# Third expert block in float32r halves, and weight conversions moved out of its steps into the second pair

## The chip, the cores and the metric

One Trainium2 chip, one of its cores. The metric is the device time of one execution in microseconds. The engines are named as the profile names them: PE (TensorE, matmuls), PEld (its weight loads), DVE (VectorE), ACT (ScalarE), POOL (GpSimd) and SP (SyncE, which here issues most transfers).

## What is computed

Clustered attention, then a mixture of eight experts with the best expert for each token, then one more pair of matmuls with a leaky ReLU:

```python
mask = q_assign[:, :, :, None] == k_assign[:, :, None, :]
attn = softmax(where(mask, q @ k.T / 8, -1e9))
x = (attn @ v) as (1536 tokens, 512)
for e in range(8):
    xe = x[expert_idx == e]
    out[expert_idx == e] = gate_w * (relu(xe @ w1[e]) @ w2[e])
h = out @ w_in
y = (relu(h) + alpha * min(h, 0)) @ w_out
```

w1 and w2 are 512x1024 and 1024x512 for each expert, w_in and w_out 512x2048 and 2048x512. All in float32.

## The kernel before, in words

The program has three stretches: attention (to about 258 us in the trace), the experts (258 to 438 us) and the second pair of matmuls (438 us to the end).

**The experts** run as 64 steps, g = 0 to 63, eight to a block. A block is one expert with a fixed number of columns (tokens), `CAPS = (208, 306, 216, 200, 192, 176, 168, 128)`. In step g the loop of line 1307 issues, in this order: `l1` of block g // 8 and slice f = g % 8 of the 1024 hidden units (four products over d), `l2` of the slice two steps back (`LAG = 2`; four products, one for each quarter o of the output), at the end of a block `y_evac` (the four sums leave PSUM), then side work of the step (a small table, lines 1117 to 1150), the entries of `ahead`, the token load of the next block (`x_load`, a transfer that ACT issues), register loads, the transposes of the next block's tokens (`x_transp`, at f = 6), and last a conversion where the table `CONV` has one. Each engine takes its instructions in this order.

**Products.** Blocks other than the second are float32: one product is two records on PE. The second block (`HB = 1`, 306 columns) is in float32r halves: each operand is a rounded high half and a low half (the rest), and `thrice` adds up high times high, high times low and low times high, three records of one pass each. The halves of the weights are made by `wsplit` two steps ahead: one ACT copy of 512 columns makes the high half, one DVE subtraction the low half, into six buffers in turn. The halves of the tokens are made in `x_transp`, those of the hidden units in `l1` (ACT ReLU, DVE subtraction out of PSUM).

**Conversions.** The weights of the second pair arrive as 64-bit floats and are turned into float32 piece by piece. A conversion of one piece (`conv_step`) is four DVE operations of 512 columns (`conv_bits`, lines 178 to 181), each working on the one before, then the store of the piece before, the ACT operation that begins the next piece (`conv_begin`, line 174), and the load of a later piece. `CONV` names the 26 steps that have one; eight of them are in steps 16 to 24. Pieces 3 to 5 are made in place: `conv_begin` of one writes into the area that the raw piece before it is still read from.

**Weights** of the experts come by `wload` through a ring of four 1 MB slots, issued by SP, after `l1` and `l2` of slices 3 and 7.

**The second pair** is 16 rounds of about 15.8 us. A round has seven products `prod` (a Strassen scheme, operands in float32r halves) and twelve groups of three matmuls (`second`, line 1393) on the round before. DVE and ACT make sums and halves of weights for the next round, activations and their halves. `xt_next(r, place)` puts work of the second half of tokens at four places of a round.

Of the kernel before, what the change touches and what calls it, by code (L numbers as in the profile page):

```python
# [21 lines left out]
P = 128  # L22
# [8 lines left out]
E = 8  # L31
# [60 lines left out]
def tile_cluster_attention_moe(ctx: ExitStack, tc: tile.TileContext, qk, kk, v, cen, cenr, gate, mw, m2w,  # L92
# [73 lines left out]
    n1, n2 = iter(range(NPW, NF)), iter(range(NF, 2 * NF))  # L166
    NEARLY = 6
    seq = [next(n2) for _ in range(NEARLY)]
    while len(seq) < 2 * NF - NPW:
        seq += [next(n2), next(n1)]  # L170
# [5 lines left out]
    def conv_bits(t, raw):  # L176
        ti = t.bitcast(I32)
        nc.vector.tensor_scalar(t, t, float(np.ldexp(1.0, -15)), None, ALU.max)
        nc.vector.tensor_scalar(ti, ti, 3, 0x3FFFFFFF, ALU.logical_shift_left, ALU.bitwise_and)
        nc.vector.scalar_tensor_tensor(ti, raw[:, :, 0], 29, ti, ALU.logical_shift_right, ALU.bitwise_or)  # L180
        nc.vector.scalar_tensor_tensor(ti, raw[:, :, 1], -0x40000000, ti, ALU.bitwise_and, ALU.bitwise_or)
# [720 lines left out]
    HB = 1  # L902
# [77 lines left out]
    def x_transp(blk, half=None):  # L980
        nt, np_ = parts(blk)
        nb = nt * np_
        xr = xrt[blk]
        if half != 1:
# [5 lines left out]
        x = xts[blk]  # L990
# [18 lines left out]
    worder = [(0, 0), (0, 1), (0, 2), (1, 0), (0, 3), (1, 1), (0, 4), (1, 2), (0, 5), (1, 3), (0, 6), (1, 4), (0, 7), (1, 5),  # L1009
              (1, 6), (1, 7)]  # L1010

    def wsplit(layer, f):
        b = wbuf[worder.index((layer, f)) % 6].rearrange("p (h d f) -> p h d f", h=2, d=4)
        w = wslots[4 * HB + 2 * (f // 4) + layer]
# [6 lines left out]
        split[layer, f] = b  # L1021

    def thrice(ps, w, i, hi, lo, start, stop):
        nc.tensor.matmul(ps, w[:, 0, i, :], hi, start=start, stop=False)  # L1024
        nc.tensor.matmul(ps, w[:, 0, i, :], lo, start=False, stop=False)  # L1025
        nc.tensor.matmul(ps, w[:, 1, i, :], hi, start=False, stop=stop)  # L1026

    def l1(blk, f):
# [6 lines left out]
        for d in range(4):  # L1035
            if blk == HB:
                thrice(ps, split[0, f], d, x[:, d, :], split["x"][:, d, :], d == 0, d == 3)
# [7 lines left out]
        if f % 4 == 3:  # L1045
            wload()

    def l2(blk, f):
# [6 lines left out]
        for o in range(4):  # L1055
            y = yps[blk][o][:, 0:nb]
            if blk == HB:
                thrice(y, split[1, f], o, h, split["h"][f % 4], f == 0, f == 7)
            else:
                nc.tensor.matmul(y, w[:, f % 4, o * P:(o + 1) * P], h, start=f == 0, stop=f == 7)  # L1060
        if f % 4 == 3:
            wload()

    def y_evac(blk, col):
        nb = CAPS[blk]
        for o, y in enumerate(yps.pop(blk)):
            dst = (x2a if o < 2 else x2b)[:, o % 2, col]
            if o % 2 == 0:
# [128 lines left out]
    def s_half(r, n):  # L1197
# [10 lines left out]
        else:  # L1208
# [22 lines left out]
    for g in range(7, 16):  # L1231
        for v in (8, 9) if g == 7 else (g + 2,):
            for layer, f in ((0, v - 8), (1, v - 10)):
                if 0 <= f < 8:
                    ahead.setdefault(g, []).append(lambda layer=layer, f=f: wsplit(layer, f))
# [423 lines left out]
```

## Time and profile before

| | us |
|---|---|
| median of 3 runs | 696.54 (695.32 to 697.29) |
| the profiled execution | 696.02 |
| its span, first to last instruction | 694.2 |
| PE busy | 679.9 (98%) |
| DVE busy | 478.9 (69%) |
| ACT busy | 378.3 (54%) |

The span has a start time for every instruction. On PE a record's duration runs past the start of the next one, so the pace of PE is read from start to start and not from the durations. On DVE and ACT an instruction's time covers its write, and the next independent one starts a little before it ends. A bracket at the end of a row is idle time ahead of the instruction and what ended it.

### The profile page before, as it was taken

What the parts mean: (1) busy time and instruction counts of PE and PEld (TensorE: products, weight loads), DVE (VectorE), ACT (ScalarE), POOL (GpSimd) and SP (SyncE); (2) the same over time, 40 slices, a digit from 0 to 9 for tenths busy, and PEclk for the clock granted to TensorE, in tenths of its full rate; (3) what the DMA queues carried; (4) which work ended last, traced back from release to release, by engine and by line L of the source; (5) the groups of instructions that cost most, each with busy time, mean ns of one, the idle gap of its engine ahead of it and who ended that gap; (6) DMA issues with size and microseconds to landing.
All of it is one profiled execution on the core that took longest, in us unless ns stands there. A gap on an engine that the chain in (4) does not pass through costs nothing.

```text
span 694.2 us, 11439 instructions
## 1 busy us (share of the span) xinstructions
PE 679.9 (98%) x4149; PEld 573.4 (83%) x4149; DVE 478.9 (69%) x885; ACT 378.3 (54%) x747; POOL 61.5 (9%) x67
## 2 busy tenths in 40 slices
PE   9999999999999999999999999999999999999994
PEld 3677667767766699999999999898899889998983
DVE  8777778777797667687747663777788765445552
ACT  6777877767776517433333443655556564334441
POOL 3220202220040130000000000000000030000003
PEclk9999999999999999999999999999999999999998
DMA  8446886633254335668999989553334565554412
GB/s 257 121 161 178 294 293 224 221 113 87 86 152 156 112 132 180 196 209 246 357 360 315 354 279 278 165 195 140 136 137 152 197 212 176 151 158 138 151 31 93
DMA packets 49145, 131.78 MB, mean 190 GB/s; under 512 B 8398, under 2 KB 14053, under 8 KB 44895
## 3 DMA queue, kind: packets, MB, share of 16 engines
q1 hardware_dynamic: 44424, 115.85, 51.1%
q0 software_dynamic: 3216, 12.60, 5.1%
q10 hardware_dynamic: 1447, 2.58, 1.5%
q8 instruction: 34, 0.56, 0.4%
q14 instruction: 24, 0.20, 0.1%
HBM read 98.15 MB, written 30.24 MB: 185 GB/s over the span
## 4 chain that ended last, share of the span: by engine, by line
PE 56%; DMA 2%; ACT 1%; DVE 1%; issue 1%; POOL 0%; POOLq 0%; ACTq 0%; DVEq 0%
PE PS L1261 16%; PE PS L1060 9%; PE PS L1039 9%; PE PS L1397 6%; PE PS L1396 6%; PE PS L1395 6%; DMA w<-in_mw 2%; PE PS L1026 1%; PE PS L1024 1%; PE PS L1025 1%; PE PS L998 1%; POOL out_dram L1408 0%; ACT gc L1377 0%; DVE SHL L1166 0%; DVE gc L1380 0%
## 5 line engine op out<-in xcount | busy, mean ns | idle before, releaser
L446 ACT ACTIVATE P<-PS,sm 128x768 f32<-128x768 f32 x96 | 86.5, 901 | 29.6 <-DVE sm L436 29.4
L436 DVE TENSOR_REDUCE sm<-PS 128x1 f32<-128x768 f32 x96 | 91.9, 957 | 14.4 <-PE PS L430 13.9
L460 PEld LDWEIGHTS PS<-cst,P 128*128 128x128 f32 x576 | 63.4, 140 | 28.7 <-ACT P L446 15.6
L460 PE MATMUL PS<-cst,P 128*128 128x128 f32 x576 | 81.7, 277 | 0.5 <-ACT PT L462 0.2
L1039 PE MATMUL PS<-x,w 128*128 128x208 f32 (+6 forms) x448 | 79.2, 320 | 0.9 <-ACT h L1041 0.9
L1060 PE MATMUL PS<-h,w 128*128 128x208 f32 (+6 forms) x448 | 79.1, 319 | 0.4 <-DMA w<-in_mw 0.4
L463 DVE COPY PT<-PS 128x384 f32<-128x384 f32 x96 | 53.0, 553 | 34.4 <-PE PS L460 34.2
L1397 PE MATMUL PS<-BH,gc 128*128 128x512 f32 x192 | 75.8, 395 | 0.0
L1396 PE MATMUL PS<-BL,gc 128*128 128x512 f32 x192 | 75.5, 393 | 0.0
L1395 PE MATMUL PS<-BH,gc 128*128 128x512 f32 x192 | 75.1, 391 | 0.0
L429 PE MATMUL PS<-KA,QA 128*128 128x512 f32 x192 | 73.6, 384 | 0.0
L1039 PEld LDWEIGHTS PS<-x,w 128*128 128x128 f32 x448 | 71.5, 190 | 1.5 <-ACT h L1041 1.2
L469 PE MATMUL PS<-PT,V 128*64 128x384 f32 (+1 forms) x432 | 72.4, 462 | 0.0
L1060 PEld LDWEIGHTS PS<-h,w 128*128 128x128 f32 x448 | 71.8, 190 | 0.6 <-DMA w<-in_mw 0.6
L1261 PE MATMUL PS<-xT,SHL 128*128 128x384 f32 x336 | 68.2, 338 | 0.2 <-DVE gc L1493 0.2
L1261 PEld LDWEIGHTS PS<-xT,SHL 128*128 128x128 f32 x336 | 59.6, 188 | 4.9 <-DVE gc L1493 0.7
L462 ACT ACTIVATE PT<-PS 128x384 f32<-128x384 f32 x96 | 46.8, 487 | 28.2 <-PE PS L460 26.6
L430 PE MATMUL PS<-KB,QB 96*128 96x512 f32 x192 | 61.1, 339 | 0.0
L1041 ACT ACTIVATE h<-PS 128x208 f32<-128x208 f32 (+7 forms) x64 | 21.4, 334 | 57.3 <-PE PS L1039 49.2
L1261 PE MATMUL PS<-xB,SHL 128*128 128x384 f32 x240 | 48.5, 337 | 0.0
L1408 POOL DMA_INDIRECT out_dram<-row,PGR x12 | 11.7, 973 | 415.6 <-ACT row L1405 406.0
L469 PEld LDWEIGHTS PS<-PT,V 128*64 128x64 f32 x432 | 25.8, 136 | 23.9 <-issue 20.7
(277 smaller groups left out, 1142.9 us busy)
## 6 DMA issues: line engine op xcount, KB each, us to landing
w<-in_mw SPq DMA_DIRECT2D x32, 1024.0 KB
SS<-SHL SPq DMA_DIRECT2D x24, 512.0 KB
SHL<-SS SPq DMA_DIRECT2D x24, 512.0 KB
raw<-in_m2w SPq DMA_DIRECT2D x20, 512.0 KB
bwr<-WB SPq DMA_DIRECT2D x16, 512.0 KB
R<-in_qk SPq DMA_DIRECT2D x7, 768.0 KB
KA<-in_kk POOLq DMA_DIRECT2D x7, 768.0 KB
Xs<-in_zeros SPq DMA_DIRECT2D x8, 614.4 KB
```

What stands on the lines that cost most here:

```text
L429: nc.tensor.matmul(ps[:, ks], st["QA"][:, hh, q0:q0 + P], st["KA"][:, hh, ks], start=True, stop=False)
L430: nc.tensor.matmul(ps[:, ks], st["QB"][0:96, hh, q0:q0 + P], st["KB"][0:96, hh, ks], start=False, stop=True)
L436: nc.vector.tensor_reduce(smt[s], psS[s % 2], AX.X, ALU.max, negate=True)
L446: nc.scalar.activation(Pt, psS[s % 2], AF.Exp, bias=smt.pop(s)[:, 0:1], accum_out=RS[:, tt, h:h + 1])
L460: nc.tensor.transpose(v4[:, kt // 3, kt % 3, :], Pt[:, kt * P:(kt + 1) * P], idf)
L469: nc.tensor.matmul(psO[64 * hh:64 * hh + 64, qs], V[:, kt, 64 * hh:64 * hh + 64], PTs[u][:, hh, kt, qs], start=kt == 0, stop=kt == KT - 1)
L1039: nc.tensor.matmul(ps, w[:, d, fs], x[:, d, :], start=d == 0, stop=d == 3)
L1060: nc.tensor.matmul(y, w[:, f % 4, o * P:(o + 1) * P], h, start=f == 0, stop=f == 7)
L1261: mm = lambda d, h, x, first, last: nc.tensor.matmul(ps, SHL[:, h, i, d, :], x[:, d, :], start=first and start, stop=last, skip_group_chec ...
L1395: nc.tensor.matmul(y, gh[n][:, i, c], whi, start=start, stop=False)
L1396: nc.tensor.matmul(y, gh[n][:, i, c], wlo, start=False, stop=False)
L1397: nc.tensor.matmul(y, gl[n][:, i, c], whi, start=False, stop=last)
```

## The change

The third block (`JB = 2`, 216 columns) is put into float32r halves too. The high and low halves of its moving operand lie side by side, so that one record of 432 columns multiplies the high weights with both, and a second record of 216 columns multiplies the low weights with the high half (`both`). The PSUM bank then holds two parts that are added outside PE, in `j1` and in `y_evac`. Six conversions leave steps 16 to 24; two are placed anew at 47 and 55, the one at 57 goes, and the last five are cut into three parts each (lines 178 and 179; 180; 181 and what follows it) and put into rounds 1 to 5 of the second pair. Expert weights of blocks 1 and 2 are loaded as soon as `wsplit` has read a slot, and the register for their address is read one step earlier. The diff, cut to its core:

```diff
+    later = [n2[13], n1[-2], n2[14], n1[-1], n2[15]]
+    seq = n2[:NEARLY]
+    for a, b in zip(n2[NEARLY:13], n1):
+        seq += [a, b]
+    seq += n1[13 - NEARLY:-2]
+    NCE_ = len(seq)
+    seq += later
...
+    def conv_part(k, i):
+        conv_bits(cvt[k], raws[k], i)
+        if i == 2:
+            conv_next(k)
...
+        if blk == JB:
+            split["j"] = [t.rearrange("p (h n) -> p h n", h=2)
+                          for t in [wq_[:, 3072:3072 + 2 * nb]] + [t[:, 1024:1024 + 2 * nb] for t in wqx]]
...
+            elif blk == JB:
+                for k in range(dn):
+                    xj = split["j"][dn * g + k]
+                    nc.scalar.activation(xj[:, 0], pv[:, k], AF.Copy)
+                    nc.vector.tensor_sub(xj[:, 1], pv[:, k], xj[:, 0].bitcast(F32))
...
+    def wsplit(blk, layer, f):
+        b = wbuf[wcount[0] % 6].rearrange("p (h d f) -> p h d f", h=2, d=4)
+        wcount[0] += 1
+        w = wslots[4 * blk + 2 * (f // 4) + layer]
...
+        split[blk, layer, f] = b
+        if f % 4 == 3:
+            wload()
...
+    def both(ps, w, i, hl, start, stop):
+        n = hl.shape[-1]
+        nc.tensor.matmul(ps, w[:, 0, i, :], hl.rearrange("p h n -> p (h n)"), start=start, stop=False)
+        nc.tensor.matmul(ps[:, 0:n], w[:, 1, i, :], hl[:, 0], start=False, stop=stop)
+
+    def j1(f):
+        nb = CAPS[JB]
+        ps = bank(f % 2)[:, 0:2 * nb]
+        for d in range(4):
+            both(ps, split[JB, 0, f], d, split["j"][d], d == 0, d == 3)
...
+        nc.scalar.activation(h, ps[:, nb:2 * nb], AF.Copy)
+        nc.vector.tensor_add(h, ps[:, 0:nb], h)
+        nc.scalar.activation(hj[:, 0], h, AF.Relu)
+        nc.vector.scalar_tensor_tensor(hj[:, 1], h, 0.0, hj[:, 0].bitcast(F32), ALU.max, ALU.subtract)
+
+    def j2(f):
...
+        for o in range(4):
+            both(yps[JB][o][:, 0:2 * nb], split[JB, 1, f], o, split["hj"][f % 3], f == 0, f == 7)
...
+            if blk == JB:
+                nc.scalar.activation(dst, y[:, nb:2 * nb], AF.Copy)
+                nc.vector.tensor_add(dst, y[:, 0:nb], dst)
...
-    CONV = {1: 1, 2: 1, 10: 1, 13: 1, 16: 1, 17: 1, 18: 1, 19: 1, 20: 1, 21: 1, 22: 1, 24: 1, 25: 1, 27: 1, 28: 1, 30: 1,
-            32: 1, 34: 1, 36: 1, 38: 1, 40: 1, 43: 1, 45: 1, 49: 1, 52: 1, 57: 1}
+    CONV = {g: 1 for g in (1, 2, 10, 13, 18, 21, 25, 27, 28, 30, 32, 34, 36, 38, 40, 43, 45, 47, 49, 52, 55)}
...
+    for b_, first_ in ((HB, ((0, 7), (1, 7))), (JB, ())):
+        for f in range(8):
+            for layer in range(2):
+                g = dict(first_).get(f, 8 * b_ + f - 2) if layer == 0 else 8 * b_ + f
+                ahead.setdefault(g, []).append(lambda a=(b_, layer, f): wsplit(*a))
...
+            (j1(f) if blk == JB else l1(blk, f))
...
+            (j2(f2) if b2 == JB else l2(b2, f2))
...
+            if f == (0 if blk else 1) and blk + 1 < NB:
+                wreg[blk + 1] = reg(wi[0:1, blk + 1:blk + 2], [ET.SP], 4 * (E - 1))
...
+    late_at = {(1, 2): (0, 0), (1, 3): (0, 1), (1, 4): (0, 2), (2, 2): (1, 0), (2, 3): (1, 1), (2, 4): (1, 2),
+               (3, 2): (2, 0), (3, 3): (2, 1), (3, 4): (2, 2), (4, 1): (3, 0), (4, 2): (3, 1), (4, 3): (3, 2),
+               (5, 1): (4, 0), (5, 2): (4, 1), (5, 3): (4, 2)}
...
     def xt_next(r, place):
+        if (r, place) in late_at:
+            n, i = late_at[r, place]
+            conv_part(NCE_ + n, i)
```

## Rows read from the trace of the kernel before

**Rows 1.** The page, busy time, share of the span and instructions of each engine.
```profile
PE 679.9 (98%) x4149; PEld 573.4 (83%) x4149; DVE 478.9 (69%) x885; ACT 378.3 (54%) x747; POOL 61.5 (9%) x67
```
**Rows 2.** Waits of PE, experts (first), second pair (second): us, times, longest.
```profile
PE PS L1039 <- ACT h L1041: 0.9, 1, 0.9
...
PE PS L1261 <- DVE gc L1493: 0.2, 1, 0.2
```
**Rows 3.** Windows, steps 10-15, 16-23, 24-26: length, PE, PEld, DVE, ACT, POOL, PEclk, DMA.
```profile
286.78:308.06 21.28, 21.28 (x154) 21.27 (x153) 17.14 (x46) 9.83 (x21) 0.00 (x0) 1.00 0.81 256
308.06:332.74 24.68, 24.68 (x147) 24.48 (x146) 19.10 (x42) 8.69 (x20) 0.00 (x0) 1.00 0.75 240
332.74:341.07 8.33, 8.33 (x49) 8.33 (x49) 5.67 (x12) 2.96 (x8) 0.00 (x0) 1.00 0.98 357
```
**Rows 4.** Timeline of PE in the third block: start, us, engine, line, operation.
```profile
323.26 1.62 PE L1039 MATMUL PS<-x,w 128*128 128x216 f32 x8
...
326.18 1.62 PE L1039 MATMUL PS<-x,w 128*128 128x216 f32 x8
```
**Rows 5.** Timeline of PE: float32r records of 256, 306, 512 columns; transposes (L460).
```profile
150.49 0.28 PE L429 MATMUL PS<-KA,QA 128*128 128x256 f32 x1
150.61 0.29 PE L430 MATMUL PS<-KB,QB 96*128 96x256 f32 x1
150.74 0.82 PE L460 MATMUL PS<-cst,P 128*128 128x128 f32 x6
151.31 0.48 PE L429 MATMUL PS<-KA,QA 128*128 128x512 f32 x1
...
290.33 0.30 PE L1024 MATMUL PS<-x,wqx 128*128 128x306 f32 x1
290.47 0.30 PE L1025 MATMUL PS<-xlo,wqx 128*128 128x306 f32 x1
...
443.22 0.40 PE L1395 MATMUL PS<-BH,gc 128*128 128x512 f32 x1
443.46 0.39 PE L1396 MATMUL PS<-BL,gc 128*128 128x512 f32 x1
```
**Rows 6.** Groups by line and form, 255 to 445 us: busy us, mean ns | idle before.
```profile
L1020 DVE TENSOR_TENSOR wq<-w,wq 128x512 fp32r<-128x512 f32 x9 | 5.9, 684 | 1.6 <-ACT wq L1019 1.5
L1019 ACT ACTIVATE wq<-w 128x512 fp32r<-128x512 f32 x9 | 5.3, 622 | 0.0
L1041 ACT ACTIVATE h<-PS 128x216 f32<-128x216 f32 x8 | 2.7, 336 | 2.1 <-PE PS L1039 2.1
L1071 DVE COPY x2a<-PS 128x216 f32 x1 | 0.4, 383 | 2.0 <-PE PS L1060 2.0
```
**Rows 7.** Timeline of DVE, step 17: a conversion, the table of step 18, the next conversion.
```profile
315.09 0.42 DVE L178 TENSOR_SCALAR wA<-wA 128x512 f32<-128x512 f32 x1
...
317.35 0.23 DVE L1144 TENSOR_TENSOR tabr<-tabr,g 11x88 f32<-11x88 f32 x1
...
318.64 0.43 DVE L178 TENSOR_SCALAR cv<-cv 128x512 f32<-128x512 f32 x1 [0.38 <-issue]
```
**Rows 8.** Timeline of ACT, DVE and PEld around the start of step 16 (308.06).
```profile
306.01 0.66 ACT L174 ACTIVATE wA<-wA 128x512 f32<-128x512 f32 x1 [5.48 <-DVE wA L181]
306.58 0.42 ACT L1041 ACTIVATE h<-PS 128x306 fp32r<-128x306 f32 x1
...
307.54 0.69 DVE L1020 TENSOR_TENSOR wq<-w,wq 128x512 fp32r<-128x512 f32 x1
308.15 0.60 DVE L1007 COPY x<-PS 128x432 f32<-128x432 f32 x1
...
308.80 0.66 PEld L1039 LDWEIGHTS PS<-x,w 128*128 128x128 f32 x4 [0.16 <-DVE x L1007]
```
**Rows 9.** Windows of DVE, second pair, a round each: length, DVE busy, PEclk, DMA share.
```profile
490.67:506.50 15.83, 11.77 (x21) 1.00 0.43 153
506.50:522.33 15.83, 13.41 (x24) 1.00 0.42 150
```

More of the change, by code (lines that the diff above doesn't have):

```diff
@@ L165, in tile_cluster_attention_moe @@
     NPW = NPRE * PRE // PCE
-    n1, n2 = iter(range(NPW, NF)), iter(range(NF, 2 * NF))
+    n1, n2 = list(range(NPW, NF)), list(range(NF, 2 * NF))
     NEARLY = 6
-    seq = [next(n2) for _ in range(NEARLY)]
-    while len(seq) < 2 * NF - NPW:
-        seq += [next(n2), next(n1)]
+    later = [n2[13], n1[-2], n2[14], n1[-1], n2[15]]
[5 more added lines that the diff above has]
+    seq += later
+    assert sorted(seq) == n1 + n2
     NCA = len(seq)
@@ L174, in conv_abs, with conv_bits @@
         nc.scalar.activation(t, raw.bitcast(F32)[:, :, 1], AF.Abs)
-    def conv_bits(t, raw):
+    def conv_bits(t, raw, i=None):
         ti = t.bitcast(I32)
[L178 to L181, printed above, removed]
+        if i in (None, 0):
+            nc.vector.tensor_scalar(t, t, float(np.ldexp(1.0, -15)), None, ALU.max)
+            nc.vector.tensor_scalar(ti, ti, 3, 0x3FFFFFFF, ALU.logical_shift_left, ALU.bitwise_and)
+        if i in (None, 1):
+            nc.vector.scalar_tensor_tensor(ti, raw[:, :, 0], 29, ti, ALU.logical_shift_right, ALU.bitwise_or)
+        if i in (None, 2):
+            nc.vector.scalar_tensor_tensor(ti, raw[:, :, 1], -0x40000000, ti, ALU.bitwise_and, ALU.bitwise_or)
     def pre_load(i):
@@ L901, in tile_cluster_attention_moe @@
     xrt, xts, yps, hts = {}, {}, {}, {}
-    HB = 1
+    HB, JB = 1, 2
     split = {}
@@ L983, in x_transp @@
         xr = xrt[blk]
-        if half != 1:
+        if half != 1 and blk != JB:
             xts[blk] = xtp.tile([P, 4, CMAX], F32R if blk == HB else F32, name=f"x_{blk}", tag="x")[:, :, 0:nb]
@@ L989, in x_transp @@
                 split["h"] = [hlo[:, CMAX * i:CMAX * i + nb] for i in range(4)]
-        x = xts[blk]
+        if blk == JB:
+            split["j"] = [t.rearrange("p (h n) -> p h n", h=2)
+                          for t in [wq_[:, 3072:3072 + 2 * nb]] + [t[:, 1024:1024 + 2 * nb] for t in wqx]]
+        x = xts.get(blk)
         dn = 2 if 2 * nb <= 512 else 1
@@ L1007, in x_transp @@
                 nc.vector.tensor_copy(x[:, dn * g:dn * (g + 1), :], pv)
[L1009 to L1014, printed above, removed]
+    wcount = [0]
+    def wsplit(blk, layer, f):
+        b = wbuf[wcount[0] % 6].rearrange("p (h d f) -> p h d f", h=2, d=4)
+        wcount[0] += 1
+        w = wslots[4 * blk + 2 * (f // 4) + layer]
         if layer == 0:
@@ L1026, in thrice @@
         nc.tensor.matmul(ps, w[:, 1, i, :], hi, start=False, stop=stop)
+    def both(ps, w, i, hl, start, stop):
[7 more added lines that the diff above has]
+            both(ps, split[JB, 0, f], d, split["j"][d], d == 0, d == 3)
+        if f == 0:
+            t = xq.tile([P, 4 * CH], F32R, name="hj", tag="x0")
+            split["hj"] = [t[:, 2 * nb * i:2 * nb * (i + 1)].rearrange("p (h n) -> p h n", h=2) for i in range(3)]
+        h = hp.tile([P, CMAX], F32, name=f"h_{JB}_{f}", tag="h")[:, 0:nb]
+        hj = split["hj"][f % 3]
+        nc.scalar.activation(h, ps[:, nb:2 * nb], AF.Copy)
[3 more added lines that the diff above has]
+    def j2(f):
+        nb = CAPS[JB]
+        if f == 0:
+            yps[JB] = [bank(4 + o) for o in range(4)]
+        for o in range(4):
+            both(yps[JB][o][:, 0:2 * nb], split[JB, 1, f], o, split["hj"][f % 3], f == 0, f == 7)
     def l1(blk, f):
@@ L1036, in l1 @@
             if blk == HB:
-                thrice(ps, split[0, f], d, x[:, d, :], split["x"][:, d, :], d == 0, d == 3)
+                thrice(ps, split[HB, 0, f], d, x[:, d, :], split["x"][:, d, :], d == 0, d == 3)
             else:
@@ L1044, in l1 @@
         hts[blk, f] = h
-        if f % 4 == 3:
+        if f % 4 == 3 and blk != HB:
             wload()
@@ L1057, in l2 @@
             if blk == HB:
-                thrice(y, split[1, f], o, h, split["h"][f % 4], f == 0, f == 7)
+                thrice(y, split[HB, 1, f], o, h, split["h"][f % 4], f == 0, f == 7)
             else:
                 nc.tensor.matmul(y, w[:, f % 4, o * P:(o + 1) * P], h, start=f == 0, stop=f == 7)
-        if f % 4 == 3:
+        if f % 4 == 3 and blk != HB:
             wload()
@@ L1230, in tile_cluster_attention_moe @@
     ahead = {g: [(lambda n=n: ahead_x(n))] for g, n in zip(range(42, 56, 2), ("T1", "T2", "T4", "T3", "B11", "B21", "B22"))}
[L1231 to L1235, printed above, removed]
+    for b_, first_ in ((HB, ((0, 7), (1, 7))), (JB, ())):
[3 more added lines that the diff above has]
+                ahead.setdefault(g, []).append(lambda a=(b_, layer, f): wsplit(*a))
     for i, g in enumerate((2, 4, 33, 37)):
```

14 lines of the change are left out of this document (7 added, 7 removed).

## The prediction

> **What bounds the kernel now.** The busy shares come first: PE is at 98%, DVE at 69%, ACT at 54% [rows 1]. A busy PE proves little, so PE's waits come next: in the whole expert stretch one wait of 0.9 us and two shorter ones, in the second pair one of 0.2 us [rows 2]. PE sets the end everywhere this change touches, and its instructions lie end to end. Two things follow. Work taken off PE is worth its full time, as long as nobody else becomes late. And moving conversions away from the third block is worth nothing by itself: DVE and ACT are not waited for there. The third view is the windows: in steps 16 to 23 (24.68 us) DVE is busy for 19.10 us, with seven conversions among it [rows 3]. The last view is the timeline at the start of step 16: PE's weight load already waits 0.16 us for the token copy that DVE finishes behind a conversion [rows 8]. Here DVE has no spare time at all.
>
> **What PE saves.** In the third block a step does eight products of 216 columns, four for each layer, in 326.18 - 323.26 = 2.92 us [rows 4], 365 ns a product. The new price is a record of 432 and one of 216 columns in float32r. The trace has float32r records of 256 columns at 0.12 us start to start, of 306 at 0.14 us, of 512 at 0.24 us [rows 5]; with the many rows around these the last two are 141 and 231 ns, 0.44 ns a column and 7 ns. That gives 198 ns at 432 (inside the measured range) and 103 ns at 216 (outside it), 301 ns a product. 64 products (eight slices, four each, two layers) save 64 x 64 ns = **4.1 us**.
> No float32r record below 256 columns is in the trace, so the 216 has bounds. From below: the transposes load new weights of 128 columns for each record at 151.31 - 150.74 = 0.57 us for six, 95 ns [rows 5]; with that 4.6 us are saved. From above: it goes as the float32 product that it replaces, 365 ns, and then PE loses 64 x 198 ns = 12.7 us. I take 103 ns, since 256, 306 and 512 columns lie on one line.
> The Trainium skill ("TensorE: Matmul & The Clock Gate", Back-to-back issue gap) gives N / 2.4 + 2.5 ns. By it the records would cost 182.5 and 92.5 ns and the saving would be an estimated 5.7 us; at 306 columns it says 130 ns where the trace has 141, so the trace decides.
>
> **What DVE and ACT get.** Prices: a split of 512 columns is 0.62 us on ACT, then 0.68 us on DVE; 216 columns out of PSUM are 0.34 us on ACT and 0.38 us on DVE [rows 6]. A following independent instruction starts 0.08 us before the end on DVE (307.54 + 0.69 against 308.15) and 0.09 us on ACT (306.01 + 0.66 against 306.58) [rows 8]. A conversion takes DVE 317.35 - 315.09 = 2.26 us [rows 7]. For a hand-over between engines I allow 0.04 to 0.05 us (an estimate, varied below).
> `j1` turns one ACT operation into a chain between the two: ACT copies the low part (0.34), DVE adds (0.38), ACT takes the ReLU (0.34), DVE subtracts (0.38), with nothing else queued between on either engine. After the ReLU come two splits. So a plain step takes DVE 0.38 add + 0.42 waiting for the ReLU + 0.30 subtraction + 0.22 waiting for ACT's first split + 2 x 0.60 = **2.5 us**. PE now needs only 8 x 301 ns = 2.4 us a step. DVE can therefore not catch up, and everything else in its queue from step 14 on delays PE once the two steps of lead are used up.
> The plain sum says the same. In steps 16 to 23 DVE was busy for 19.1 us [rows 3]; five conversions go (5 x 2.23 = 11.2, without the gaps), 14 splits and 16 operations of 216 columns come (9.5 + 6.1 = 15.6): 23.5 us. PE's work falls from 24.7 us by 56 of the 64 products, 3.6 us, to 21.1. Overlaps of 0.08 us at some 50 operations bring DVE down to about 19.4, and eight times the 0.42 + 0.22 us of waiting up to 24.5: more than PE's 21.1.
>
> I laid the three queues out in the order of the program from step 10 to step 27, each instruction starting when its engine and its operands are free. For the kernel before this gives 53.9 us, without a wait of PE; the trace has 21.28 + 24.68 + 8.33 = 54.29 us [rows 3], and DVE's operations lie within 0.3 us of the trace. For the changed one it gives these waits of PE (times on the scale of the trace):
> - Step 16, **1.2 us.** Behind the 0.69 us subtraction of 307.54, in place of one copy of 432 columns at 308.15 [rows 8], DVE has the first split of the new block (0.60) and then four subtractions of 216, the first done at 309.1. PE wanted it at 308.1. ACT's splits and copies stand behind the same conversion of step 13: ACT waited 5.48 us for it [rows 8].
> - Step 20, **0.8 us.** DVE has the adds of steps 16, 17, 18 at 311.35, 314.09, 317.28: in step 17 two `y_evac` copies (0.8), in step 18 the table (0.9). The low half of split (first layer, slice 4) ends at 320.5; PE wants it at 319.6.
> - Step 21, **3.8 us.** The conversion of step 18 lies on DVE from 320.8 to 323.1 (0.38 us of register load before it [rows 7]). It is piece 4, and the ACT operation that begins piece 5 overwrites its raw data, so ACT waits for its end, as in the 5.48 us of [rows 8]. Queued behind that on ACT are copy and ReLU of slice 3 and then the split for slice 5: high half at 326.0, low half at 326.8. PE wanted both at 322.8.
> - Step 24, **1.2 us.** The conversion of step 21 delays the add of slice 6 to 334.0, hence the ReLU, hence ACT's copy of the next block's tokens (done 335.7, wanted at 334.7).
> - Small ones, 0.1 us.
>
> Together **7.1 us of waits against 4.1 us of work: 3.0 us slower**. Bounds: with all hand-overs at 0.03 us, no cost for register loads and the ends of all durations 0.02 to 0.04 us lower it is 1.2 us slower; with hand-overs at 0.1 us and the token load of step 17 at 0.9 us on ACT instead of 0.4, 4.7 us.
> `y_evac` of the new block (four copies and four adds of 216 instead of two and two) lies behind the four products of step 26, and costs nothing in that layout.
>
> **The other moves.** The earlier `wload` of blocks 1 and 2 moves six to eight transfers up SP's queue; they then wait for DVE's split, which holds back the conversion stores and raw loads queued behind. Each has 15 us until it is read; nothing. Steps 16 to 24 lose six conversions, where none was waited for: nothing. New conversions at 47 and 55 and none at 57: `y_evac` of step 57 has 0 to 0.5 us more ahead of it; I take nothing.
> In rounds 1 to 5 DVE is busy 11.8 us of 15.83, in round 5 13.4 us [rows 9]; a conversion adds 2.26 us of DVE and 0.66 us of ACT, plus a store and in two rounds a load on SP. Round 5 comes to 15.7 us of busy time, but each of its 28 operations overlaps its neighbour by 0.08 us, so some 13.4 us of occupancy. The same layout for these rounds gives no wait of PE; it takes conversions of one and a half times the length before PE waits 1.7 us. So nothing, with 0 to 1.5 us as bounds. The last stores (rounds 4 and 5) are needed by `b_load` at the end of those rounds, for weights that are used a round later: hidden.
>
> **The sum.** 696.02 us of the profiled execution + 3.0 = 699.0; that execution lies 0.5 us below the median of 696.54, so **699.5 us** for the median. PE's granted clock is 1.00 in these windows [rows 3, 9] and I keep it there.
>
> **The rivals.**
> 1. *The queues keep up* (faster). If DVE and ACT recover between the conversions, only PE's work counts: 696.5 - 4.1 = **692.4 us**. For it: the second block makes the same splits, with two conversions beside them, and PE waits for DVE only 0.16 us at its end [rows 8]. Against it: a step there is 3.4 us of PE and not 2.4, and has no chain between ACT and DVE. Chance 0.12.
> 2. *Waits and gain cancel*: the wait of step 21 is the largest; if ACT is not held there (3.2 us less), the sum is -0.2 us, **696.3 us**; without the waits of steps 16 and 24 it is 0.6 us slower. Within 0.3%, which is about what a measurement of this kernel can tell from no change, is 694.5 to 698.6. Chance 0.22.
> 3. *The 216-column record costs as much as the float32 product.* PE then needs 4.5 us a step and waits only in step 16: 12.7 + 1.2 = 13.9 us, **710.4 us**. It decides from about 170 ns on. For it: no narrower row than 256 columns. Chance 0.08.
> 4. *The second pair waits too*: 1.5 us on top of the forecast, **701 us**; in the forecast's range.
>
> **How the numbers follow.** The forecast, waits larger than the gain, 697.7 to 701.2 us (1.2 and 4.7 us; with rival 4 a little more), has 0.58. Range: leaving out rival 3 (0.08) and most of rival 1, 694.0 to 702.5. Faster by over 0.3%: 0.13 (rival 1 and a little of rival 2). Within: 0.21 + 0.08 of the forecast's lower end = 0.29. Slower: 0.50 + 0.08 = 0.58.
>
> **What the profile after would show.** Right: in the third block PE records of 432 and 216 columns at 0.20 and 0.10 us start to start; PE idle for some 7 us in steps 16 to 24, the longest for an ACT split of step 21 behind the operation that begins a conversion, itself waiting for DVE; steps 16 to 23 longer than 24.7 us by about 2.5 us; no wait of PE in rounds 1 to 5. Wrong: steps 16 to 23 in 21 us without waits (rival 1), or the 216-column records at over 0.17 us (rival 3), or waits of PE behind DVE in rounds 4 and 5 (rival 4).

## The result, and the profile of the changed kernel

The changed kernel takes 700.1 us (median of 7 runs, 698.6 to 703.59) where the kernel before takes 696.5 us beside it (7 runs, 695.32 to 697.29): ratio 1.0068, 95% interval 1.0046 to 1.0089. It is slower by 3 to 6 us, as forecast (699.5). Its profiled execution took 702.62 us, a long one among its runs.

| us | before | changed |
|---|---|---|
| span of the profiled execution | 694.2 | 700.8 |
| steps 10 to 15 | 21.28 | 21.30 |
| steps 16 to 23 | 24.68 | 30.34 |
| steps 24 to 26 | 8.33 | 7.89 |

Steps 10 to 26 are 5.24 us longer. (Step 10 begins at 287.67, step 24 at 339.31, step 27 at 347.20; step 16 counts from 308.97, where PE had done the step before it.) The page has the busy time of each engine:

```profile
PE 681.8 (97%) x4149; PEld 571.8 (82%) x4149; DVE 493.8 (70%) x922; ACT 389.7 (56%) x776; POOL 60.9 (9%) x67
```

Beside [rows 1], DVE has 14.9 us more and ACT 11.4. PE has 1.9 us more, although its new products are shorter: the first sign that something slowed PE itself. PE's waits from 255 to 445 us (in total, times, longest), against [rows 2]:

```profile
PE PS L1057 <- ACT wq L1044: 2.5, 1, 2.5
PE PS L1057 <- DVE wq L1028: 0.9, 1, 0.9
...
PE PS L1093 <- ACT cv L179: 0.5, 1, 0.5
PE PS L1057 <- DVE wqx L1028: 0.5, 2, 0.2
PE PS L1058 <- DVE wqx L1045: 0.4, 1, 0.4
```

L1057 and L1058 are the records of 432 and 216 columns, L1044 and L1045 the two halves of a weight, L1028 the low half of the tokens. The 2.5 us belong to step 21, 0.9 and 0.5 to step 16, 0.4 to step 20: 4.4 us in the third block. Step 24 has no wait. The 0.5 us for `h` lie ahead of step 8, as the 0.9 us of [rows 2] do. The 0.5 us put down to ACT's `cv` are at 422.33, ahead of the first product of block 7; what was late there is open, since e5 has the same work of ACT at this place and no wait. The second pair has two waits of 0.2 us, one of which the kernel before has too. The windows, with columns as in [rows 3], are cut just before step 16's first record (310.07), at step 21's first record and at the end of the slow stretch:

```profile
287.67:309.83 22.16, 21.45 (x154) 21.20 (x152) 18.00 (x48) 10.03 (x21) 0.00 (x0) 1.00 0.74 233
309.83:327.88 18.05, 14.37 (x89) 12.99 (x89) 14.07 (x34) 10.41 (x26) 0.00 (x0) 0.99 0.46 156
327.88:334.20 6.32, 6.24 (x21) 5.52 (x21) 5.04 (x13) 3.96 (x9) 0.00 (x0) 0.50 0.46 167
```

Here is what the forecast did not have: after the wait of 2.54 us PE's granted clock is 0.50 for 6.32 us, the lower of its two levels (1.2 instead of 2.4 GHz). The timeline of PE shows a product at either level:

```profile
318.24 0.38 PE L1057 MATMUL PS<-hj,wq 128*128 128x432 f32 x1
318.45 0.27 PE L1058 MATMUL PS<-hj,wq 128*128 128x216 f32 x1
318.56 0.37 PE L1057 MATMUL PS<-hj,wq 128*128 128x432 f32 x1
...
327.88 0.73 PE L1057 MATMUL PS<-wq 128*128 128x432 f32 x1 [2.54 <-ACT wq L1044]
...
329.03 0.60 PE L1057 MATMUL PS<-wqx,wq 128*128 128x432 f32 x1
329.43 0.38 PE L1058 MATMUL PS<-wqx,wq 128*128 128x216 f32 x1
329.61 0.59 PE L1057 MATMUL PS<-wqx,wq 128*128 128x432 f32 x1
```

From start to start a product is 0.21 + 0.11 us at the full clock (0.31 over several), and 0.40 + 0.18 us at the lower level. The wait itself, in the timelines of DVE and then of ACT:

```profile
324.33 0.69 DVE L189 SCALAR_TENSOR_TENSOR wA<-wA 128x512 int32<-128x512 int32 x1
325.99 0.38 DVE L1071 TENSOR_TENSOR h<-PS,h 128x216 f32<-128x216 f32 x1 [0.97 <-ACT h L1070]
...
325.06 0.66 ACT L179 ACTIVATE wA<-wA 128x512 f32<-128x512 f32 x1 [3.70 <-DVE wA L189]
325.62 0.33 ACT L1070 ACTIVATE h<-PS 128x216 f32<-128x216 f32 x1
326.40 0.38 ACT L1072 ACTIVATE hj<-h 128x216 fp32r<-128x216 f32 x1 [0.45 <-DVE h L1071]
326.69 1.13 ACT L1044 ACTIVATE wq<-w 128x512 fp32r<-128x512 f32 x2
```

The conversion of step 18 ends on DVE at 325.02. ACT's L179, which begins piece 5, waited 3.70 us for it. Behind it stand copy, ReLU and the split that PE waits for.

Another place is the second pair, which the forecast had at nothing. DVE, then PE, timelines of the changed kernel:

```profile
527.94 0.68 DVE L189 SCALAR_TENSOR_TENSOR cv<-raw,cv 128x512 int32<-128x512 int32 x1
...
531.41 0.55 DVE L1542 TENSOR_TENSOR gc<-PS,gc 128x384 f32<-128x384 f32 x1
...
532.02 1.33 PE L1317 MATMUL PS<-xT,SHL 128*128 128x384 f32 x6 [0.18 <-DVE gc L1542]
```

The first line is the last part of the last moved conversion. DVE is busy without a gap from it to the addition that PE waits for. From start to start PE loses 0.47 us here, in every trace with the moved conversions (the changed kernel and all runs but e7), and nothing in the two without them (the kernel before and e7).

### The profile page after: what moved, and what is told of

Its sections match the earlier page's. It is cut to its first block, busy times and chain, and to the rows that moved or that the text cites. A ratio compares the mean times of both kernels' runs of the same rounds, so it can differ in the third digit from the quotient of the medians.

```text
span 700.8 us, 11507 instructions
## 1 busy us (share of the span) xinstructions
PE 681.8 (97%) x4149; PEld 571.8 (82%) x4149; DVE 493.8 (70%) x922; ACT 389.7 (56%) x776; POOL 60.9 (9%) x67
## 4 chain that ended last, share of the span: by engine, by line
PE 51%; DVE 5%; ACT 3%; issue 2%; POOL 0%; POOLq 0%; DVEq 0%; ACTq 0%
PE PS L1317 14%; PE PS L1093 8%; PE PS L1114 8%; PE PS L1455 5%; PE PS L1454 5%; PE PS L1453 5%; PE PS L1057 1%; PE PS L1053 1%; PE PS L1051 1%; PE PS L1052 1%; PE PS L1018 1%; PE PS L1058 1%; ACT gc L1435 1%; DVE wq L1045 1%; DVE wqx L1045 1%
## 5 line engine op out<-in xcount | busy, mean ns | idle before, releaser
L1093 PE MATMUL PS<-x,w 128*128 128x208 f32 (+5 forms) x384 | 66.2, 316 | 1.0 <-ACT h L1095 0.5
L1114 PE MATMUL PS<-h,w 128*128 128x208 f32 (+5 forms) x384 | 66.0, 315 | 0.0
L1093 PEld LDWEIGHTS PS<-x,w 128*128 128x128 f32 x384 | 59.9, 190 | 1.6 <-ACT h L1095 0.9
L1114 PEld LDWEIGHTS PS<-h,w 128*128 128x128 f32 x384 | 60.1, 190 | 0.0
L1095 ACT ACTIVATE h<-PS 128x208 f32<-128x208 f32 (+6 forms) x56 | 18.6, 332 | 59.9 <-PE PS L1093 52.0
L1317 PEld LDWEIGHTS PS<-xB,SHL 128*128 128x128 f32 x240 | 42.9, 188 | 3.1
```

The lines of the kernel that those rows point to most:

```text
L1093: nc.tensor.matmul(ps, w[:, d, fs], x[:, d, :], start=d == 0, stop=d == 3)
L1317: mm = lambda d, h, x, first, last: nc.tensor.matmul(ps, SHL[:, h, i, d, :], x[:, d, :], start=first and start, stop=last, skip_group_chec ...
```

## The experiments

Besides the median, each is read by stage: from the start of step 8's first ReLU to the end of the span (282.66 to 694.2 before, 283.54 to 700.8 changed). This leaves out what varies ahead of step 8 from one execution to the next (the last section tells of one cause). Each figure comes from one execution, and two things in it have nothing to do with the third block. PE's last product is done 8.8 to 9.6 us before the end, a spread of 0.8 us. And the trace of the kernel before has a wait of its own:

```profile
430.40 1.16 PE L1060 MATMUL PS<-h,w 128*128 128x128 f32 x8 [0.40 <-DMA w<-in_mw]
```

It costs 0.66 us from start to start, and e7, with the same experts and second pair, does not have it. So differences below some 0.7 us say little by themselves. Each median of the kernel before was taken together with that of the run beside it.

| kernel | median | before | ratio (95%) | step 8 to end, against before |
|---|---|---|---|---|
| changed | 700.1 | 696.5 | 1.0068 (1.0046 to 1.0089) | +5.7 |
| e1 | 696.12 | 695.61 | 0.9993 (0.9966 to 1.0020) | +0.4 |
| e2 | 695.48 | 695.61 | 0.9997 (0.9973 to 1.0022) | -2.6 |
| e3 | 700.66 | 695.61 | 1.0079 (1.0051 to 1.0107) | +4.2 |
| e4 | 697.27 | 695.61 | 1.0027 (1.0001 to 1.0052) | -0.1 |
| e5 | 698.92 | 695.52 | 1.0045 (1.0025 to 1.0064) | +2.0 |
| e6 | 699.89 | 695.52 | 1.0053 (1.0028 to 1.0078) | +2.4 |
| e7 | 694.79 | 695.52 | 0.9991 (0.9974 to 1.0009) | -0.6 |
| e8 | 694.64 | 695.52 | 0.9972 (0.9950 to 0.9994) | -1.9 |
| e9 | 698.92 | 695.23 | 1.0053 (1.0034 to 1.0073) | (below) |
| e10, e8 again | 694.61 | 695.23 | 0.9982 (0.9963 to 1.0001) | -2.0 |
| e11 | 692.70 | 695.23 | 0.9961 (0.9941 to 0.9980) | -3.4 |
| e12 | 698.46 | 695.89 | 1.0027 (1.0004 to 1.0051) | +4.1 |

### e1 and e2: the conversions beside the block

```diff
-    CONV = {g: 1 for g in (1, 2, 10, 13, 18, 21, 25, 27, 28, 30, 32, 34, 36, 38, 40, 43, 45, 47, 49, 52, 55)}
+    # e1
+    CONV = {g: 1 for g in (1, 2, 10, 13, 24, 25, 26, 27, 28, 30, 32, 34, 36, 38, 40, 43, 45, 47, 49, 52, 55)}
+    # e2
+    CONV = {g: 1 for g in (1, 2, 10, 24, 25, 26, 27, 28, 30, 31, 32, 34, 36, 38, 40, 43, 45, 47, 49, 52, 55)}
```

> The changed kernel with the conversions of steps 18 and 21 moved to steps 24 and 26; nothing else. Theory A (DVE's queue with the conversions in it makes PE late, and the 2.5 us wait of step 21 makes the granted clock fall to 0.50 for 6.3 us): the wait of step 21 shrinks from 2.5 to under 0.6 us, the clock stays at 1.00 in steps 21 to 23, steps 16 to 23 take about 25 us instead of 29.5, and the time is within 1 us of the kernel before (696.5), some 4 us under the changed one. Rival B (the loss is in the float32r products or in the earlier weight loads): no change, 700 us. Rival C (the five conversions in the second pair cost it): no change, 700 us, with waits of PE after 445 us.

> As the run before, and the conversion of step 13 moved too: conversions at 24, 26 and 31 in place of 13, 18 and 21. Theory A: the wait at the start of step 16 (1.4 us in three pieces) goes as well, since DVE and ACT reach the halves of the tokens in time; steps 16 to 23 take about 22 us, and the time is 2.9 us below the kernel before, 693.6 us: two thirds of the 4.1 us that PE's records save. Rival B: 700 us. If PE waits in steps 24 to 32 instead, the conversions only moved their cost, and it comes out at 696 us or more.

Without the conversions of steps 18 and 21, the wait of step 21 is gone and those of steps 16 and 20 stand as they were (1.0, 0.5 and 0.4 us); by stage the kernel is level with the one before (+0.4): the third block is 0.5 us shorter, and two waits for weights and the second pair take that back. Without that of step 13 too, the waits of steps 16 and 20 go as well, PE has no wait in the third block, and the stage is 2.6 us shorter. So these three conversions make the waits, and step 20's is left over from step 13's. The window of e2 from step 16's first record to step 24's (columns as in [rows 3]):

```profile
310.55:332.46 21.91, 21.83 (x147) 20.88 (x145) 17.24 (x41) 13.43 (x33) 0.00 (x0) 1.00 0.67 190
```

The kernel before needs 24.7 us for the same stretch and the changed one 29.24. With steps 24 and 25, which still have products of the block, e2's is 3.2 us shorter than the one before: this is what the new products save where nothing waits. Against e2, record by record, the changed kernel comes later by 2.2 us in step 16, 0.4 in step 20, 3.3 at the start of step 21 (2.7 up to its first record, 0.6 up to the second, which needs the low half of the weight; e5 has a wait of 0.35 us for DVE there) and 2.5 in the rest of the stretch at the lower clock. That is 8.4 us; less 3.2, it is the 5.2 us that steps 10 to 26 are longer. A wait costs more than the idle time in its bracket, because a record's duration runs past the next start.

e2's median does not follow its stage (-0.1 us, interval -1.9 to +1.5): that question led to e7 to e12.

### e3: work for PE in the wait

```diff
+            if g == 21:
+                warm(11, bank(2))
```

Eleven bf16 products of 512 columns that nobody reads.

> The changed kernel with eleven added matmuls of 512 columns in bfloat16 (0.215 us each, into a bank that nobody reads) on PE at the start of step 21, where it waits for 2.5 us. Nothing is left out. Theory A: the wait becomes work, so PE does not stop, the granted clock stays at 1.00 in steps 21 to 23, and 2 to 3 us that the half clock cost come back; some 1 us of that goes to the wait of step 24 that the slow steps had covered: 1.5 to 2.5 us under the changed kernel, about 698 us. Rival B (the clock falls for another reason, or costs nothing because DVE is late anyway): no change, 700 us.

PE in e3, timeline, and a window over the stretch (columns as in [rows 3]):

```profile
329.23 2.32 PE L288 MATMUL PS<-oneb 128*128 128x512 bf16 x10
331.71 0.47 PE L1057 MATMUL PS<-wq 128*128 128x432 f32 x1 [0.16 <-ACT wq L1044]
...
332.72 0.37 PE L1057 MATMUL PS<-wqx,wq 128*128 128x432 f32 x1
...
333.03 0.37 PE L1057 MATMUL PS<-wqx,wq 128*128 128x432 f32 x1
```
```profile
332.00:334.00 2.00, 1.66 (x11) 1.46 (x11) 1.51 (x6) 1.21 (x3) 0.00 (x0) 1.00 0.45 82
```

The clock stays at 1.00, and the products have their 0.31 us at once. From step 16 to step 26 that is worth 1.4 us, about half of the 2.5 us that the lower clock took: with a faster PE, step 24 waits 0.8 us for ACT instead of not at all. (By stage it is 1.5 us, +4.2 against +5.7, but the tail behind PE's last product has its part in that.) The median shows no gain (700.66, 0.8% above the kernel before, where the changed kernel was 0.7% above it). So that the wait brings the lower clock is shown; that filling it shortens the kernel is read from a single execution, and the ten times do not confirm it.

### e4: the conversions moved, the block as before

```diff
-    CONV = {1: 1, 2: 1, 10: 1, 13: 1, 16: 1, 17: 1, 18: 1, 19: 1, 20: 1, 21: 1, 22: 1, 24: 1, 25: 1, 27: 1, 28: 1, 30: 1,
-            32: 1, 34: 1, 36: 1, 38: 1, 40: 1, 43: 1, 45: 1, 49: 1, 52: 1, 57: 1}
+    CONV = {g: 1 for g in (1, 2, 10, 13, 18, 21, 25, 27, 28, 30, 32, 34, 36, 38, 40, 43, 45, 47, 49, 52, 55)}
...
+        if (r, place) in late_at:
+            n, i = late_at[r, place]
+            conv_part(NCE_ + n, i)
```

> The kernel before (third block in float32) with the other half of the change alone: the new table of steps for the conversions, and the last five in rounds 1 to 5 of the second pair. Theory A: no change, 696.5 us within 0.5 us, as PE waits for DVE neither in the third block nor in the rounds. Rival C (DVE is full in rounds 4 and 5): 1 to 2 us slower, with waits of PE in the rounds. Rival D (conversions beside the third block cost PE something that the waits do not show): faster by over 1 us.

The third block is as long as before (24.66 us for steps 16 to 23): taking conversions away from it is worth nothing by itself, as the prediction said. In the second pair PE loses the 0.47 us shown above. That the stage comes out at -0.1 us is due to the kernel before, whose trace has its own 0.66 us. The median is 0.1 to 3.6 us above the kernel before; the profiled execution had lost 1.75 us ahead of step 8, which the edit does not touch (the last section). So the moved conversions cost 0.47 us where they were put; that they cost something elsewhere is not excluded.

### e5: ACT not held behind the conversion

```diff
-        conv_begin(k + 1)
+        if k != 4:
+            conv_begin(k + 1)
...
+        if g == 20:
+            conv_begin(5)
```

> The changed kernel, with only the op that begins piece 5 (ScalarE's multiply that waits for the conversion of step 18) moved from the middle of step 18 to the end of step 20, behind ScalarE's work for steps 18 to 20. Theory A (ScalarE is held in order behind that op, 3.70 us in the changed kernel, and the halves of the weight for step 21 come late for it): the 2.5 us wait at the start of step 21 falls to about 2, a part of it being VectorE's own lateness from its two conversions; 0.5 to 1.1 us less from step 8 to the end, about 699.3 against 700.1. Rival (VectorE's conversions alone are late, the order on ScalarE is beside the point): the wait stays at 2.5 us and the time at 700.1.

ACT, and then PE, timeline of e5:

```profile
321.43 0.33 ACT L1071 ACTIVATE h<-PS 128x216 f32<-128x216 f32 x1
325.51 0.38 ACT L1073 ACTIVATE hj<-h 128x216 fp32r<-128x216 f32 x1 [3.75 <-DVE h L1072]
...
326.98 0.46 PE L1058 MATMUL PS<-wq 128*128 128x432 f32 x1 [1.49 <-ACT wq L1045]
```

The copy goes through at 321.43, but now the ReLU waits 3.75 us: for DVE's add, which stands behind the same conversion. The wait of step 21 falls from 2.54 to 1.49 us, more than expected, and not to nothing. The clock stayed at 1.00 in the block, and step 24 waits 0.84 us for ACT. By stage e5 is 3.7 us shorter than the changed kernel; 2.3 us of that lie in steps 16 to 26, the rest behind them. The medians of e5 and of the changed kernel (698.9 and 700.1) lie in the same direction; their intervals overlap.

### e6: both copies ahead of the subtractions

```diff
+                xj = split["j"][dn * g:dn * (g + 1)]
                 for k in range(dn):
-                    xj = split["j"][dn * g + k]
-                    nc.scalar.activation(xj[:, 0], pv[:, k], AF.Copy)
-                    nc.vector.tensor_sub(xj[:, 1], pv[:, k], xj[:, 0].bitcast(F32))
+                    nc.scalar.activation(xj[k][:, 0], pv[:, k], AF.Copy)
+                for k in range(dn):
+                    nc.vector.tensor_sub(xj[k][:, 1], pv[:, k], xj[k][:, 0].bitcast(F32))
```

> The changed kernel, with the order of the four ops turned that make halves of two token tiles of the third block: both copies of ScalarE first, then both subtractions of VectorE. Theory A (ScalarE's copy of the second tile waits until VectorE has read the first one's tile, because both lie in one bank of PSUM and the order of the program is kept): ScalarE's waits of 0.90 and 0.50 us before its copies at steps 15 and 16 go, TensorE's waits of step 16 fall from 0.95 + 0.24 + 0.22 to about 0.9, and the time falls by about 0.5 us. Rival (VectorE is the late one, and turning the order only moves the wait): TensorE's waits of step 16 keep their sum of 1.4 us, no change in time.

The changed kernel's timeline of ACT and DVE at this place, then that of e6 (ACT, PE) and its windows after step 21:

```profile
308.81 0.34 ACT L1027 ACTIVATE wq<-PS 128x216 fp32r<-128x216 f32 x1
310.05 0.59 ACT L1027 ACTIVATE wqx<-PS 128x216 fp32r<-128x216 f32 x2 [0.90 <-DVE wq L1028]
311.14 0.35 ACT L1027 ACTIVATE wqx<-PS 128x216 fp32r<-128x216 f32 x1 [0.50 <-DVE wqx L1028]
...
309.64 0.38 DVE L1028 TENSOR_TENSOR wq<-PS,wq 128x216 fp32r<-128x216 f32 x1
```
```profile
307.03 0.34 ACT L1027 ACTIVATE wq<-PS 128x216 fp32r<-128x216 f32 x1
307.26 0.83 ACT L1027 ACTIVATE wqx<-PS 128x216 fp32r<-128x216 f32 x3
...
308.28 0.46 PE L1058 MATMUL PS<-wq,wqx 128*128 128x432 f32 x1 [0.94 <-DVE wq L1029]
```
```profile
326.00:328.00 2.00, 2.00 (x8) 1.91 (x9) 1.55 (x5) 1.42 (x3) 0.00 (x0) 0.50 0.84 279
328.00:330.00 2.00, 2.00 (x11) 1.91 (x11) 1.20 (x4) 1.46 (x4) 0.00 (x0) 0.75 0.60 250
```

ACT's second copy had waited until DVE had read the first tile of the same PSUM bank; with the order turned the four copies go through at once, and step 16 keeps its 0.94 us and loses the two pieces of 0.24 and 0.22. These are the 0.5 us expected; from start to start it is 1.0 us. The stage is 3.3 us shorter than in the changed kernel, and not by the edit alone: the same wait of 2.5 us is followed here by about 3 us at the lower clock instead of 6.3, which is 1.0 us less lost; 0.2 lie in step 20, 0.6 at step 56 and 0.4 behind PE's last product. How long the clock stays down differs between these two executions. The median (699.9) is that of the changed kernel.

### e7: the additions that GpSimd holds up

```diff
-            for k in range(self.n):
-                nc.vector.tensor_add(ohsum, ohsum, OH[:, self.t0 + k, :])
-                yield
+            n = self.t0 + self.n
+            with nc.allow_low_precision(reason="whole numbers up to 24"):
+                nc.vector.tensor_reduce(ohsum, OH[:, 0:n, :].rearrange("p t e -> p e t"), AX.X, ALU.add)
+            yield
```

> The kernel before, with the three additions of 8 counts at the end of a routing group replaced by one reduction over the counts so far. Theory C (the spread of single executions ahead of the change comes in part from these additions, which stand 3.70 us instead of 0.49 us when they start beside GpSimd's subtraction of 3.6 us at 202.5 us): in each profiled execution the attention around 203 us goes through without a hole of TensorE, the median falls by 0 to 1 us below the kernel before, and fewer executions lie above 697. Rival (the spread arises elsewhere): median and spread as before, 695.6 with single executions to 700.

0.7 us less in the median, with an interval that includes none; 1 execution of 10 lies above 697, of the kernel before 8 of 28. In line with the theory, and not more, as far as the median goes. That the reduction goes through while GpSimd subtracts is in e10's trace (the last section).

### e8 and e10: the three edits together

e2, e6 and e7 in one kernel.

> The changed kernel with three edits: the conversions of steps 13, 18 and 21 moved to the second pair (24, 26, 31), the copies of ScalarE ahead of VectorE's subtractions for the token halves, and the one reduction of e7. Theory A: no wait of TensorE over 0.1 us in the third block, 2.6 to 3.0 us less than the kernel before from step 8 to the end, so about 2.8 us less than e7_one_sum on the same chip and 692.5 in all. Rival (the saving is given back in the second pair or is no more than the spread): within 1 us of e7_one_sum.

> e8 once more, for comparison with e9 and e11 on one chip. Theory D: 0.5 to 2 us less than the kernel before, with single executions over a range of 4 us, as the weights come late by more or less. Rival: 2.8 us less than the kernel before, in which case the small distance between e8 and e7 was spread.

The medians are 0.9 and 0.6 us below the kernel before, one interval below 1 and one that touches it. By stage -1.9 and -2.0 us, against -0.6 for e7. No wait is left in the third block. But each has one or two new ones, for weights: PE of e8, timeline, then its window of that stretch (columns as in [rows 3]):

```profile
374.11 1.43 PE L1095 MATMUL PS<-x,w 128*128 128x176 f32 x8 [1.27 <-DMA w<-in_mw]
```
```profile
360.00:380.00 20.00, 18.73 (x121) 18.30 (x120) 14.10 (x25) 6.56 (x15) 0.00 (x0) 1.00 1.04 354
```

The queues are full there, and PE now comes to the weights before they do.

### e9, e11 and e12: the weights as the next limit

```diff
     # e9
-    CONV = {g: 1 for g in (1, 2, 10, 24, 25, 26, 27, 28, 30, 31, 32, 34, 36, 38, 40, 43, 45, 47, 49, 52, 55)}
+    CONV = {g: 1 for g in (1, 2, 6, 8, 9, 10, 25, 27, 28, 30, 32, 34, 36, 38, 40, 43, 45, 47, 49, 52, 55)}
     # e11
-            raws[k] = raw_tile(cvp, f"raw_{k}")
-        nc.sync.dma_start(raws[k].rearrange("p n t -> p (n t)"), m2i[seq[k]])
+            if k < NEARLY + 3:
+                kept[k % 3] = raw_tile(cvp, f"raw_{k}")
+            raws[k] = kept[k % 3]
+        if k < NEARLY + 3:
+            nc.sync.dma_start(raws[k].rearrange("p n t -> p (n t)"), m2i[seq[k]])
     # e12
+    CONV = {g: 1 for g in (1, 2, 10, 25, 27, 28, 30, 32, 34, 36, 38, 40, 43, 45, 47, 49, 51, 52, 54, 55, 58)}
```

> As e8, but with the three conversions of steps 13, 18 and 21 put at steps 6, 8 and 9 instead of 24, 26 and 31. Theory D (the saving of e8 is given back to the stream of weights: from 340 to 420 us the queues are at 0.94 to 1.04 of their time, and three more loads of 512 KB and their stores stand there): no wait of TensorE for a weight's DMA over 0.5 us, 1.0 to 1.5 us less than e8 again in this call, about 2.9 us less than the kernel before. Rival (VectorE at steps 6 to 10 has no room for three times 2.9 us): new waits of TensorE of 1 us and more at steps 7 to 11, and the time of e8 or more.

> As e8, but the loads of the pieces to be converted stop after the ninth: the later conversions work on the last three pieces loaded, so that 12 loads of 512 KB are left out, 6 MB of the stretch from step 24 on. That part of the result is not the reference's. Theory D: no wait of TensorE for a weight's DMA from 340 to 440 us, and 1 to 1.5 us less than e8 again in the median. Rival (the queues aren't what keeps the gain): within 0.5 us of e8 again.

> As e8, but the three conversions go to steps 51, 54 and 58 (and that of step 52 stays) instead of 24, 26 and 31, so that every conversion of the second pair begins as many loads later and the first half of that stretch has as few loads of pieces as the changed kernel. Theory D: the weights of the first half (360 to 380 us) are no longer late, 0.5 to 1.0 us less than e8, about 693.8 against 694.6 where the kernel before has 695.2; three conversions come due where VectorE idles from 420 to 428 us. Rival (the queues are as full at 400 to 430 us, so that the lateness only moves there, to the last weights): within 0.4 us of e8 again, with a wait for a weight's DMA after 400 us.

Windows of the kernel before, and of e11, for the stretch shown of e8; then PE of e12 in its second half, timeline and window:

```profile
360.00:380.00 20.00, 20.00 (x129) 19.88 (x128) 15.92 (x27) 7.35 (x16) 0.00 (x0) 1.00 1.01 328
```
```profile
360.00:380.00 20.00, 20.00 (x131) 19.98 (x130) 15.22 (x26) 6.68 (x15) 0.00 (x0) 1.00 0.77 243
```
```profile
425.32 2.05 PE L1095 MATMUL PS<-x,w 128*128 128x128 f32 x8 [3.44 <-DMA w<-in_mw]
```
```profile
425.30:428.00 2.70, 2.68 (x12) 2.70 (x13) 0.00 (x0) 0.28 (x1) 0.00 (x0) 0.50 1.06 432
```

e11, which leaves out the later raw loads (and so computes something else), settles it: the queues are at 0.77, no weight is late, the stage is 3.4 us shorter than before and the median 1.9 us below that of e10, measured beside it. The queues were full in the kernel before too (1.01), but there PE comes to these weights later. e12 moves the lateness instead of ending it: nothing is late up to 410 us, then PE waits 0.62, 0.31 and 3.44 us for weights, and the last is followed by the lower clock. e9 went the rival's way: its conversions beside the second block make PE wait 2.0 us at 282.9 and 0.96 at 297.8 for ACT's splits and 1.3 at 303.6 for DVE's. (Part of this lies ahead of the first ReLU of step 8, so it has no stage figure.) None of the three places tried takes three more conversions for nothing.

## Why the prediction was right, step by step

The forecast (slower, 699.5 us) and its reason, DVE and ACT late beside three conversions, held: e1 and e2 take the conversions away, and the waits go with them. The size of the parts differs, and one step failed. The sizes below are those against e2.

- **What PE saves.** The 216-column record takes 0.10 us, the value chosen and not the upper bound, which ends the third rival. The 432-column one takes 0.21 instead of 0.198. At 0.31 us a product 64 of them save 64 x 55 ns = 3.5 us; in e2 the whole block is 3.2 us shorter. Forecast: 4.1. (The lower bound of 95 ns was none: it takes six transposes up to the next group's start, while from one to the next they are 0.11 us apart.)
- **Step 16**: 2.2 us, forecast 1.2. That DVE and ACT come late from step 13's conversion is shown by e2. The alternation in one PSUM bank, 1.0 us of it (e6), was not in the layout: it had the four subtractions wait for DVE alone, and took no order among readers of a bank.
- **Step 20**: 0.4, forecast 0.8. **Step 24**: nothing, forecast 1.2; here the slower PE had given DVE and ACT time, and at the full clock the wait is there (0.76 us in e3, 0.84 in e5).
- **Step 21**: 3.3, forecast 3.8, at the named instruction. But ACT's hold is only 1.05 us of it (e5). The second rival took 3.2 us away with the hold; DVE's add behind the conversion would have held ACT all the same.
- **"PE's granted clock is 1.00 and I keep it there"** is the step that failed. The wait brought the lower level for 6.32 us and cost 2.5 us more in the profiled execution, of which e3 gives back 1.4 net.
- **The other moves** at nothing: the moved conversions cost 0.47 us behind round 5, by the fourth rival's mechanism and at a third of its price.
- **The sum** of the profiled execution: 5.9 us of waits and 2.5 of clock, less 3.2, are 5.2 us. The forecast had 7.1 less 4.1. Too much wait and too much saving nearly balanced (2.7 us against 3.0), and the clock came on top, so the right total rests in part on luck. The profiled execution is also a long one, 2.5 us above the median. One of the seven has a mean granted clock of 0.997 (the profiled one 0.992). 6.32 us at 0.50 take 0.0045 off that mean, so this one had no such stretch; it took 700.1 us, the median itself, more than any of the seven of the kernel before. So the loss does not hang on the clock alone. Over all executions the mean granted clock is 0.9933 in the changed kernel and 0.9931 in e6, against 0.9955 in e2, in e3 and in the kernel before beside these two.
- **The first rival's** 692.4 us is met only in appearance by e11's 692.7: the kernel before beside it has 695.2, and e11 has e7's reduction too. With no wait in the third block and no late weight, the median is 2.5 us lower, and not 4.1. The prediction named DVE and ACT as what stands in the way; the weights behind them it had taken as having 15 us to spare.

## What to carry to other kernels

When PE's work shrinks, lay out the order of every engine that feeds it, and price each wait twice: as time, and as what PE's clock may lose after it. An instruction held in order behind a long one is rarely alone; ask what stands on the other engine behind the same one before counting its removal. And moving side work takes its transfers along: look at the DMA share where it lands.

## What the runs showed of the hardware

**The clock after a wait.** Waits of 2.54 us (changed kernel, e6) and 3.44 us (e12) were followed by a granted clock of 0.50, for 6.32, about 3 and about 3 us; a wait of 1.49 us (e5) and a wait filled with other products (e3) were not. Nor is it the length alone: of two nearly equal holes of PE in the attention, 2.78 us in e2 and 2.72 us in e3, the first left the clock at 1.00 and the second was followed by 0.50 and 0.58 over 3.7 us. So a wait of this size brings a cost that differs between executions. And a wait is not the only thing that the lower level follows: in e4, e5 and e9 the clock falls near 249 us for about 3 us though PE's records there stand end to end, while the kernel before and the changed one keep 1.00 in this stretch. Windows of e4 (columns as in [rows 3]):

```profile
248.00:250.00 2.00, 2.00 (x21) 1.97 (x21) 1.85 (x10) 0.71 (x2) 1.62 (x4) 0.73 0.36 136
250.00:252.00 2.00, 2.00 (x23) 1.35 (x19) 0.76 (x6) 0.00 (x0) 0.00 (x0) 0.50 0.34 132
```

**Two readers of one PSUM bank.** ACT and DVE read different columns of one bank one after the other: 0.90 and 0.50 us of ACT's time, gone when the order was turned (e6). The Trainium skill ("PSUM — Partial Sum Buffer", PSUM bank collisions raise a hardware error) says that the compiler adds a dependency between instructions of different engines on one bank and the same partitions, reads among themselves too; the trace agrees. That it is the bank and not the tile in it was not tested apart.

**DVE held by GpSimd.** Three additions of 8 columns stand 3.70 us in e2 instead of 0.49. DVE, GpSimd and PE of e2, then DVE and GpSimd of the kernel before (timelines):

```profile
202.40 3.70 DVE L603 TENSOR_TENSOR ohsum<-ohsum,OH 128x8 bf16<-128x8 bf16 x3
...
202.51 3.57 POOL L336 TENSOR_TENSOR KA<-R,KA 64x768 fp32r<-64x768 f32 x2 [4.02 <-DMA KB<-E]
...
206.62 0.55 PE L477 MATMUL PS<-cst,P 128*128 128x128 f32 x3 [2.78 <-DVE PT L480]
```
```profile
202.42 0.49 DVE L586 TENSOR_TENSOR ohsum<-ohsum,OH 128x8 bf16<-128x8 bf16 x3
...
203.57 3.60 POOL L319 TENSOR_TENSOR KA<-R,KA 64x768 fp32r<-64x768 f32 x2 [5.06 <-DMA KB<-E]
```

When GpSimd's subtraction begins within the additions, DVE stands until GpSimd is done, and PE then waits 2.78 us; when a transfer lands 1 us later, nothing happens. e2, e3 and e4 had this in their profiled executions (additions of 3.70, 3.62 and 2.06 us; waits of PE of 2.8, 2.7 and 1.2 us), the other kernels with the additions not: one source of spread, in work that the change does not touch. The Trainium skill ("SBUF — State Buffer", Who interferes with whom) says that a DVE instruction with two inputs in SBUF contends with a GpSimd one that reads SBUF, and calls the shared ports an exclusive lock; the trace agrees. The same section of the Trainium skill has it that a reduction on DVE never contends with GpSimd on this chip; e10's trace agrees, where the reduction began within the subtraction and took 0.12 us:

```profile
203.01 3.61 POOL L336 TENSOR_TENSOR KA<-R,KA 64x768 fp32r<-64x768 f32 x2 [3.79 <-DMA KB<-E]
203.14 0.12 DVE L604 TENSOR_REDUCE ohsum<-OH 128x8 bf16<-128x24 bf16 x1
```
